# Reordering the start of a chunked linear recurrence in a fused attention and mixture-of-experts kernel

## The chip, the cores and the metric

The kernel runs on one core of a Trainium2 chip. The metric is the device time of one execution in microseconds (us). The engines are named as in the profile: PE is the matrix engine (PEld its weight loads), DVE the vector engine, ACT the scalar engine, POOL the GpSimd engine, SP the engine whose queue issues most DMAs. Each engine works through its own list of instructions strictly in order and waits on semaphores for the others.

## The reference, cut to what matters

Four batches with eight heads give 32 independent recurrences over 768 steps, with a 40x40 state each. The result, laid out as 3072 tokens of 320 features, goes through a top-1 mixture of eight experts.

```python
def _attn_ref(r, k, v, w, a, b):
    for t in range(768):
        y[:, :, t] = einsum('bhd,bhde->bhe', rt, state)
        Sa = einsum('bhde,bhe->bhd', state, at)
        state = state * wt[:, :, None, :] - einsum('bhd,bhe->bhde', Sa, bt)
        state = state + einsum('bhd,bhe->bhde', vt, kt)

def _moe_ref(x, w_gate, w_output_gate, w1, w2):
    e_idx = argmax(x @ w_gate); gate_w = softmax(x @ w_gate)[e_idx]
    eom = sigmoid(x @ w_output_gate)
    for e in range(8):
        out[mask_e] = gate_w * eom * (relu(x[mask_e] @ w1[e]) @ w2[e])
```

## The kernel before, in words

The 768 steps are cut into 12 chunks of 64 (C). Inside a chunk the recurrence is a triangular system, so each chunk needs a preparation that doesn't depend on the state, an inverse of its triangular matrices, and then a sequential part that takes the state in and hands it on. The 32 heads lie as two sides of 16 (NP).

`scan(c)` (L104) loads the decays w of chunk c by a DMA on SP (L110), squares them on ACT for a range check (L112), and runs two prefix products P and I on DVE (L116), a reciprocal (L118) and a scaling of I (L120). `prep(c)` (L128) loads a, k and b (D, L135), forms the decayed Av on DVE (L176, L177, and two columns on ACT, L178), sends strips of it into LA by DMA (L171), forms KBt on DVE (L183), and copies Wp on ACT (L187). Then, for each of the two sides, it makes three masked copies Am of Av (for chunk 0 all six on DVE, L198; for the others on ACT, L200), and for three groups of that side multiplies them by KBt on PE (L206) into a PSUM tile pl. From each pl, ACT copies the LA part (L210), POOL cuts it to a triangle (L212), and two copies fill the two halves of N (L218: for chunk 0 the first half on DVE, otherwise both on ACT). After that come Nm (L165) and transposes of KBt and Wp on PE with copies on ACT (L155, L157). The tile Am has one buffer, or for side 1 of chunk 0 one of KB's; LA and KB have four buffers, so preparation of chunk c+4 waits for chunk c's readers.

`tinv(cs)` (L226) inverts the triangular blocks: transposes of N on DVE (L241, or L246 for pairs of chunks), a chain of multiply and reduce pairs on DVE (L251, L253, L287, L292, L295) each of which needs the one before, a last transpose (L303, or L308), and for the first four chunks (FAST) two copies Tc on ACT (L305). Chunks 0 to 3 are inverted singly, the others in pairs.

`crit(c, q)` (L339) is the sequential part for half q of the heads: the products of LA with the state (L350), masked moves on ACT (L354), applications of Tc, Nm and N on PE (L363) with additions on DVE (L376), the copies into XU on ACT (L393, L394), and the new state (L401 to L410), which is scaled by Dt, a product of LA of this chunk and of the next on POOL (L380). `tail` (L413) forms the outputs, and `route` and `pick` (L604, L625) the choice of expert. After the last chunk the experts run (L827).

What sets the order: the program is traced once in Python, a planner gives each instruction a priority by its place in that trace, and lays out every engine's list with its own estimates of when each instruction becomes ready, picking the ready instruction of highest priority. The trace order comes from `run` (L469). Its generator `background` traces scan 0, then for each batch of chunks prep, the next chunk's scan, and tinv; `need(c)` advances it until chunk c's inverse is traced, and four steps of it (RATE) are traced per step of `crit`:

```python
s.warm(s.ident, 40)
s.scan(0)
for b in batches:
    yield from preps(b)      # prep(c), then scan(c + 1)
    if b == batches[0]:
        first()              # loads of the router weights
    yield from inv(b)        # tinv(b)
```

`need(min(c + 1, n - 1))` (L522) stands ahead of crit(c, 0), so preparation and inverse of chunk 1 and the scan of chunk 2 are traced ahead of the sequential part of chunk 0.

Of the kernel before, what the change touches and what calls it, by code (L numbers as in the profile page):

```python
# [20 lines left out]
C = 64  # L21
NP = 16
# [32 lines left out]
class Att:  # L55
    npool = 0

    def __init__(s, ctx, tc, ident, win, din, rl, vl, vt, nch=12):
        s.tc, s.nc, s.nch, s.ident = tc, tc.nc, nch, ident
        s.win, s.din, s.rl, s.vl, s.vt = win, din, rl, vl, vt  # L60
        nc = s.nc
        pool = lambda n, b, **k: ctx.enter_context(tc.tile_pool(name=n, bufs=b, **k))
        s.cp, s.p2, s.p5 = (pool(f"p{i}", i) for i in (1, 2, 5))
        s.ps = pool("ps", 1, space=PSUM)
        s.dr = pool("dr", 2, space=DRAM)
        s.pre = ExitStack()
        s.p1 = s.pre.enter_context(tc.tile_pool(name="p0", bufs=1))
        s.mM = s.cp.tile([128, C], F32, name="mM")
        nc.gpsimd.memset(s.mM, 1.0)
        for h in range(2):  # L70
            nc.gpsimd.affine_select(out=s.mM[64 * h:64 * h + 64], in_=s.mM[64 * h:64 * h + 64], pattern=[[1, C]],
                                    base=0, channel_multiplier=-1, compare_op=ALU.is_gt, fill=0.0)

        s.mj = s.cp.tile([120, 3], F32, name="mj")
        nc.gpsimd.memset(s.mj, -1.0)
        for j in range(3):
            m = s.mj[:, j:j + 1]
            nc.gpsimd.affine_select(out=m, in_=m, pattern=[[0, 1]], base=-40 * j, channel_multiplier=1,
                                    compare_op=ALU.is_ge, fill=0.0)
            nc.gpsimd.affine_select(out=m, in_=m, pattern=[[0, 1]], base=40 * j + 39, channel_multiplier=-1,  # L80
                                    compare_op=ALU.is_ge, fill=0.0)
        s.rst = s.p1.tile([120, 792], BF16, name="rst")
        nc.gpsimd.memset(s.rst, 0.0)
        nc.gpsimd.memset(s.rst[:, 0:792:33], 1.0)
        s.Tt = s.p1.tile([128, 1056], F32, name="Tt")
        nc.gpsimd.memset(s.Tt, 0.0)
        nc.gpsimd.memset(s.Tt[:, 0:1056:33], 1.0)


        s.hm = s.cp.tile([128, 2], F32, name="hm")  # L90
        nc.vector.tensor_reduce(out=s.hm, in_=s.ident.rearrange("p (x h s) -> p h x s", x=4, h=2), axis=AX.XY, op=ALU.add)
        s.hq = s.cp.tile([128, 2], F32, name="hq")
        nc.vector.tensor_reduce(out=s.hq, in_=s.ident.rearrange("p (x h s) -> p h x s", x=2, h=2), axis=AX.XY, op=ALU.add)
        s.wb = s.cp.tile([120, 1], F32, name="wb")
        nc.gpsimd.memset(s.wb, -0.9)
        s.wsq = s.cp.tile([120, nch], F32, name="wsq")
        s.rqm = s.cp.tile([120, nch], F32, name="rqm")
        s.zb = s.cp.tile([128, 32], F32, name="zb")
        nc.gpsimd.memset(s.zb, 0.0)
        s.buffers()  # L100
        s.st, s.ld, s.post, s.idle = {}, {}, [], False


    def scan(s, c):  # L104

        nc, V = s.nc, s.nc.vector
        n = 12 * 2 * 33
        w = s.p1.tile([120, n + 1], F32, name="w")
        V.memset(w[:, n:], 0.0)
        nc.sync.dma_start(out=w[:, 0:n], in_=s.win[c])  # L110
        sq = s.p1.tile([120, 24, 32], BF16, name="sq")
        nc.scalar.activation(out=sq, in_=pat(w, 1, [(33, 24), (1, 32)]), func=AF.Square, bias=s.wb, accum_out=s.wsq[:, c:c + 1])  # L112
        P, I = (s.p1.tile([120, 12, 2, 33], F32, name=x) for x in "PI")
        Pf, If = (x.rearrange("p r h t -> p (r h t)") for x in (P, I))
        for o, d in ((Pf, w[:, 0:n]), (If[:, ::-1], w[:, n:0:-1])):
            V.tensor_tensor_scan(out=o, data0=d, data1=s.rst, initial=0.0, op0=ALU.mult, op1=ALU.add)  # L116
        rq = s.p1.tile([120, 24], F32, name="rq", bufs=2)
        V.reciprocal(out=rq, in_=P[:, :, :, 32])  # L118
        I3 = I.rearrange("p r h t -> p (r h) t")
        V.tensor_tensor(out=I3, in0=I3, in1=rq.unsqueeze(2).broadcast_to([120, 24, 33]), op=ALU.mult)  # L120
        s.Q = P, I, rq
# [6 lines left out]
    def prep(s, c):  # L128
# [60 lines left out]
        for side in range(2):  # L189
# [4 lines left out]
            else:  # L194
                Am = s.p1.tile([120, 3, 6, C], F32, name="Am", tag="Am")
            for j in range(3):
                if c == 0:
                    V.tensor_scalar(out=Am[:, j], in0=As_[:, :, 0:64], scalar1=s.mj[:, j:j + 1], scalar2=None, op0=ALU.mult)  # L198
                else:
                    nc.scalar.activation(out=Am[:, j], in_=As_[:, :, 0:64], func=AF.Copy, scale=s.mj[:, j:j + 1])  # L200
            yield
            for g0 in range(0, 6, 2):
                pl = s.ps.tile([128, 2, 3, C], F32, name="pl", tag="pl" if c or g0 == 0 else "tl", bufs=2 if c or g0 == 0 else 3)
                nj = 3 if g0 < 4 else 2
                for i in range(2):
                    nc.tensor.matmul(pl[:, i, 0:nj], KBt[:, 6 * side + g0 + i].rearrange("p n t -> p (n t)"), Am[:, 0:nj, g0 + i],  # L206
                                     start=True, stop=True)
                pv = pl.rearrange("p g j t -> p j g t")
                la = pat(LA[64:128, side], 66 * g0, [(396, nj), (66, 2), (1, 64)])
                nc.scalar.copy(out=la, in_=pv[0:64, 0:nj])  # L210
                for i in range(2):
                    g.affine_select(out=la[:, :, i], in_=la[:, :, i], pattern=[[0, nj], [1, C]], base=0, channel_multiplier=-1,  # L212
                                    compare_op=ALU.is_gt, fill=0.0)
                for h in range(2):
                    r = slice(64 * side + 32 * h, 64 * side + 32 * h + 32)
                    n = C - 32 * h
                    nn = pat(N[r], C * g0, [(6 * C, nj), (C, 2), (1, n)])
                    (V.tensor_copy if c == 0 and not h else nc.scalar.copy)(out=nn, in_=pv[64 + 32 * h:96 + 32 * h, 0:nj, :, C - n:])  # L218
                yield
        split()  # L220
        for side in range(2):
# [4 lines left out]
    def tinv(s, cs):  # L226
# [73 lines left out]
            s.st[c]["Tc"] = s.Tp[:, c % 2]  # L300
        if fast:
            Th = tmp[:, 512:1024].rearrange("p (n x t) -> p n x t", x=2, t=16)
            V.transpose(out=pat(Th, 0, [(1, 16), (16, 2), (32, NP)]), in_=pat(Tt, 0, [(1, 16), (0, 2), (32, 16)]))  # L303
            for x in range(2):
                nc.scalar.activation(out=s.st[cs[0]]["Tc"][:, :, 16 * x:16 * x + 16], in_=Th[:, :, x], func=AF.Copy,  # L305
                                     scale=s.hm[:, x:x + 1])
# [162 lines left out]
    def run(s, sink, first, then=None):  # L469
# [17 lines left out]
        def background():  # L487
            s.warm(s.ident, 40)
            s.scan(0)
            for b in batches:  # L490
                yield from preps(b)
                if b == batches[0]:
                    first()
                yield from inv(b)
            s.pre.close()
            s.idle = True
            if then:
                yield from then()
# [551 lines left out]
```

## Time and profile before

| | us |
|---|---|
| median of 3 runs | 797.86 |
| lowest and highest | 795.27, 801.42 |
| profiled execution | 804.69 |
| its span, first to last instruction | 803.0 |

All instruction times are those of the profiled execution, counted from the start of its span; 1.69 us of its time lie outside the span. In the timeline view, a line is a start, a duration, the engine, the source line, the operation, what it writes and reads, how many instructions were merged, and in brackets the idle time of that engine just before and what ended it. A group of merged instructions lasts from the first start to the last end.

### The profile page before, as it was taken

What the parts mean: (1) busy time and instruction counts of PE and PEld (TensorE: products, weight loads), DVE (VectorE), ACT (ScalarE), POOL (GpSimd) and SP (SyncE); (2) the same over time, 40 slices, a digit from 0 to 9 for tenths busy, and PEclk for the clock granted to TensorE, in tenths of its full rate; (3) what the DMA queues carried; (4) which work ended last, traced back from release to release, by engine and by line L of the source; (5) the groups of instructions that cost most, each with busy time, mean ns of one, the idle gap of its engine ahead of it and who ended that gap; (6) DMA issues with size and microseconds to landing.
All of it is one profiled execution on the core that took longest, in us unless ns stands there. A gap on an engine that the chain in (4) does not pass through costs nothing. (4 is left out here: it accounts for less than half of the span.)

```text
span 803.0 us, 22193 instructions
## 1 busy us (share of the span) xinstructions
PE 687.7 (86%) x9378; PEld 616.9 (77%) x9378; DVE 472.2 (59%) x921; ACT 386.9 (48%) x871; POOL 231.2 (29%) x334
## 2 busy tenths in 40 slices
PE   5767987876898798889999968978999999999992
PEld 5656767765787687778888867767899998988992
DVE  7877766257952568946975954335467454455220
ACT  1576684665325783765387323424356253353210
POOL 9541223313112234452132320022534223311101
PEclk9555699999779988997999989898999999999997
DMA  7653334244222544364431554206557335332001
GB/s 173 149 119 81 95 89 105 72 99 108 69 56 57 116 105 106 93 130 96 100 83 46 112 123 126 62 13 171 173 169 215 120 106 184 108 93 67 16 9 28
DMA packets 61152, 81.13 MB, mean 101 GB/s; under 512 B 34226, under 2 KB 48373, under 8 KB 59606
## 3 DMA queue, kind: packets, MB, share of 16 engines
q1 hardware_dynamic: 57206, 70.74, 35.1%
q0 software_dynamic: 3840, 8.91, 3.8%
q8 instruction: 76, 1.25, 0.7%
q14 instruction: 30, 0.25, 0.1%
HBM read 67.59 MB, written 8.96 MB: 95 GB/s over the span
## 5 line engine op out<-in xcount | busy, mean ns | idle before, releaser
L212 POOL TENSOR_SCALAR_AFFINE_SELECT LA<-LA 64x192 f32<-64x192 f32 x144 | 69.7, 511 | 148.0 <-ACT LA L210 141.6
L206 PE MATMUL pl<-Am,KBt 120*128 120x192 f32 (+1 forms) x288 | 71.4, 396 | 24.6 <-ACT Am L200 16.4
L773 DVE SCALAR_TENSOR_TENSOR hl<-ph,hh 128x480 fp32r<-128x480 f32 (+1 forms) x76 | 41.7, 562 | 68.1 <-ACT hh L772 65.1
L768 PE MATMUL ph<-xh,w1h 128*128 128x480 f32 (+1 forms) x228 | 79.5, 353 | 2.3 <-DVE hl L773 1.3
L206 PEld LDWEIGHTS pl<-Am,KBt 120*128 120x128 f32 x288 | 56.8, 239 | 30.1 <-ACT Am L200 18.0
L781 PE MATMUL po<-w2h,hh 128*120 128x320 f32 x256 | 78.7, 312 | 1.1 <-ACT hh L772 1.1
L772 ACT ACTIVATE hh<-ph 128x480 fp32r<-128x480 f32 (+1 forms) x76 | 36.7, 498 | 88.6 <-PE ph L768 79.4
L768 PE MATMUL ph<-xl,w1h 128*128 128x480 f32 (+1 forms) x228 | 78.5, 347 | 0.0
L782 PE MATMUL po<-w2l,hh 128*120 128x320 f32 x256 | 77.6, 309 | 0.0
L783 PE MATMUL po<-w2h,hl 128*120 128x320 f32 x256 | 74.8, 310 | 0.0
L786 POOL DMA_INDIRECT out_dram<-y,ti x32 | 34.0, 1061 | 141.8 <-DVE y L785 75.8
L354 ACT ACTIVATE As<-pa,hq 128x320 f32<-128x320 f32 x88 | 46.3, 529 | 46.9 <-PE pa L363 33.8
L363 PE MATMUL pa<-As,Tc 64*32 64x40 f32 x2048 | 59.0, 212 | 9.5 <-ACT As L354 5.6
L363 PEld LDWEIGHTS pa<-As,Tc 64*32 64x32 f32 x2048 | 48.1, 118 | 20.6 <-ACT As L354 8.2
L452 PE MATMUL pY<-KB,M 128*64 128x40 f32 x768 | 57.3, 238 | 7.4 <-POOL M L443 4.3
L451 PE MATMUL pY<-Sd,R 128*64 128x40 f32 x704 | 57.1, 240 | 3.1 <-ACT LG L616 3.1
L435 PE MATMUL pM<-R,VU 128*128 128x128 f32 x384 | 57.3, 302 | 1.8 <-ACT VU L427 1.7
L452 PEld LDWEIGHTS pY<-KB,M 128*64 128x64 f32 x768 | 50.0, 147 | 9.7 <-POOL M L443 4.5
L218 ACT COPY N<-pl 32x192 f32<-32x192 f32 (+1 forms) x138 | 49.9, 362 | 10.1 <-PE pa L363 7.7
L687 POOL DMA_INDIRECT tab<-rec,si x24 | 25.5, 1063 | 99.0 <-DVE rec L684 49.9
L435 PEld LDWEIGHTS pM<-R,VU 128*128 128x128 f32 x384 | 51.2, 210 | 3.5 <-ACT VU L427 2.1
L451 PEld LDWEIGHTS pY<-Sd,R 128*64 128x64 f32 x704 | 48.3, 146 | 6.6 <-ACT LG L616 3.3
(192 smaller groups left out, 1645.2 us busy)
## 6 DMA issues: line engine op xcount, KB each, us to landing
D<-in_din_dram SPq DMA_DIRECT2D x12, 1080.0 KB
st<-in_w_dram SPq DMA_DIRECT2D x16, 512.0 KB
st<-in_w_dram SPq DMA_DIRECT2D x16, 480.0 KB
XS<-in_vt_dram SPq DMA_DIRECT2D x24, 256.0 KB
XU<-in_vt_dram SPq DMA_DIRECT2D x24, 256.0 KB
VU<-in_vl_dram SPq DMA_DIRECT2D x24, 208.0 KB
w<-in_win_dram SPq DMA_DIRECT2D x12, 371.2 KB
st<-in_w_dram SPq DMA_DIRECT2D x16, 256.0 KB
```

The costliest lines, as they stand in the source:

```text
L206: nc.tensor.matmul(pl[:, i, 0:nj], KBt[:, 6 * side + g0 + i].rearrange("p n t -> p (n t)"), Am[:, 0:nj, g0 + i], start=True, stop=True)
L212: g.affine_select(out=la[:, :, i], in_=la[:, :, i], pattern=[[0, nj], [1, C]], base=0, channel_multiplier=-1, compare_op=ALU.is_gt, fill=0.0)
L218: (V.tensor_copy if c == 0 and not h else nc.scalar.copy)(out=nn, in_=pv[64 + 32 * h:96 + 32 * h, 0:nj, :, C - n:])
L354: nc.scalar.activation(out=x, in_=pa, func=AF.Copy, scale=s.hq[:, h:h + 1])
L363: nc.tensor.matmul(pa[o + w:o + w + 32, i], m(p)[o:o + 64], x[o:o + 64, i, :], start=start, stop=True, tile_position=(o, o + w), skip_grou ...
L435: nc.tensor.matmul(pM[:, i], VU[:, h0 + i].rearrange("p n t -> p (n t)"), R[:, :, h0 + i], start=True, stop=True)
L451: nc.tensor.matmul(o, R[:, side, i, :], Sd[:, i, :], start=True, stop=False)
L452: nc.tensor.matmul(o, Ms[i // 4][:, i % 4, side, :], KB[:, side, p, :], start=not c, stop=True)
L768: nc.tensor.matmul(ph, l, r, start=(i == 0), stop=(i == 7))
L781: nc.tensor.matmul(po, hh[f][:, ts_], w2h[:, f], start=(f == 0), stop=False)
L782: nc.tensor.matmul(po, hh[f][:, ts_], w2l[:, f], start=False, stop=False)
L783: nc.tensor.matmul(po, hl[f][:, ts_], w2h[:, f], start=False, stop=(f == 7))
```

## The change

`issue_after(ins)` makes each instruction traced in its block that runs on the engine of `ins` stand behind `ins` in that engine's list; it adds no wait and binds no other engine. `high_priority()` lets what is traced in it go ahead of all else that is ready.

The change traces prep(0) and tinv(0) under high priority, and the scan of chunk 1 and the router's loads only after them. The three masks of side 1 of chunk 0 go from DVE to ACT. Each scan's DVE instructions get a place to stand behind: scan 1 stands behind the last DVE copy of chunk 0's N; scans 2 to 5 stand behind the last DVE transpose of the inverse of chunks 0 to 3. In every chunk and group N's two copies are traced ahead of the copy into LA.

```diff
@@ Att.__init__
-        s.st, s.ld, s.post, s.idle = {}, {}, [], False
+        s.st, s.ld, s.post, s.idle, s.mark = {}, {}, [], False, {}
     def scan(s, c):
+        with s.tc.issue_after(s.mark[c]) if c in s.mark else ExitStack():
+            s.scan_(c)
+    def scan_(s, c):
@@ prep
             for j in range(3):
-                if c == 0:
+                if c == 0 and not side:
                     V.tensor_scalar(out=Am[:, j], in0=As_[:, :, 0:64], scalar1=s.mj[:, j:j + 1], ...)
                 else:
                     nc.scalar.activation(out=Am[:, j], in_=As_[:, :, 0:64], func=AF.Copy, scale=s.mj[:, j:j + 1])
@@
+                for h in range(2):
+                    r = slice(64 * side + 32 * h, 64 * side + 32 * h + 32)
+                    n = C - 32 * h
+                    nn = pat(N[r], C * g0, [(6 * C, nj), (C, 2), (1, n)])
+                    pn = pv[64 + 32 * h:96 + 32 * h, 0:nj, :, C - n:]
+                    if c == 0 and not h:
+                        s.mark[1] = V.tensor_copy(out=nn, in_=pn).ins
+                    else:
+                        nc.scalar.copy(out=nn, in_=pn)
                 nc.scalar.copy(out=la, in_=pv[0:64, 0:nj])
                 for i in range(2):
                     g.affine_select(out=la[:, :, i], ...)
-                for h in range(2):
...
-                    (V.tensor_copy if c == 0 and not h else nc.scalar.copy)(out=nn, ...)
@@ tinv
-            V.transpose(out=pat(Th, ...), in_=pat(Tt, ...))
+            s.mark[cs[0] + 2] = V.transpose(out=pat(Th, ...), in_=pat(Tt, ...)).ins
@@ run, background
             s.scan(0)
-            for b in batches:
+            for g in (s.prep(0), s.tinv([0])):
+                while True:
+                    with s.tc.high_priority():
+                        if next(g, done) is done:
+                            break
+                    yield
+            ready[0] = True
+            s.scan(1)
+            first()
+            for b in batches[1:]:
                 yield from preps(b)
-                if b == batches[0]:
-                    first()
                 yield from inv(b)
```

## Rows read from the trace of the kernel before

**Rows 1.** The page's busy times of the engines over the whole span, and the granted clock of PE in 40 equal slices of 20 us (tenths of full speed).
```profile
PE 687.7 (86%) x9378; PEld 616.9 (77%) x9378; DVE 472.2 (59%) x921; ACT 386.9 (48%) x871; POOL 231.2 (29%) x334
...
PEclk9555699999779988997999989898999999999997
```

**Rows 2.** Busy time of each engine by stretch: stretch, its length, then for each engine the busy us and the count, the granted clock, the DMA share and GB/s. The stretches are from the first mask product to the end of chunk 0's Tc, from there to chunk 0's first XU copy, and from there to the last XU copy.
```profile
20.30:58.70 38.40, 26.66 (x136) 21.70 (x136) 28.78 (x51) 24.65 (x64) 18.91 (x30) 0.50 0.62 139
58.70:87.30 28.60, 20.68 (x273) 17.66 (x274) 20.67 (x50) 19.83 (x48) 4.93 (x12) 0.56 0.26 65
87.30:525.00 437.70, 378.08 (x7202) 333.31 (x7202) 282.06 (x580) 241.23 (x577) 111.34 (x170) 0.90 0.39 94
```

**Rows 3.** Timeline of DVE from 17 to 40 us: chunk 0's masks, scan 1, chunk 1's KBt, the first transpose of inverse 0.
```profile
17.25 7.36 DVE L198 TENSOR_SCALAR Am<-Av,mj 120x384 f32<-120x384 f32 x6
24.54 1.79 DVE L116 TENSOR_TENSOR_SCAN P<-w,rst 120x792 f32<-120x792 f32 x1
26.25 1.88 DVE L116 TENSOR_TENSOR_SCAN I<-w,rst 120x792 f32<-120x792 f32 x1
...
31.98 0.98 DVE L120 TENSOR_TENSOR I<-I,rq 120x792 f32<-120x792 f32 x1
...
38.25 0.95 DVE L183 TENSOR_TENSOR KBt<-D,I 120x768 f32<-120x768 f32 x1
39.12 1.09 DVE L241 STREAM_TRANSPOSE tmpf<-N 128x512 f32<-128x512 f32 x1
```

**Rows 4.** The view of line 198 alone: duration of one mask on DVE, least, median and greatest, in ns.
```profile
L198 DVE TENSOR_SCALAR Am<-Av,mj x6: 401/1390/2087, 17.2 to 24.2; 120x384 f32<-120x384 f32 x6
```

**Rows 5.** Timeline of POOL beside these masks: three clears of LA for later chunks.
```profile
18.08 5.99 POOL L139 MEMSET LA<- 32x2112 f32 x3
```

**Rows 6.** Timeline of ACT: the Square of scan 1, the LA copies behind it, the last copies of chunk 0's N and of chunk 1's N, the masks of chunk 2 and Tc of chunk 0.
```profile
23.81 0.94 ACT L112 ACTIVATE sq<-w,wb 120x768 bf16<-120x768 f32 x1 [7.38 <-DMA w<-in_win_dram]
...
24.86 0.85 ACT L210 COPY LA<-pl 64x384 f32<-64x384 f32 x2
...
37.24 0.47 ACT L218 COPY N<-pl 32x192 f32<-32x192 f32 x2
...
55.60 0.63 ACT L218 COPY N<-pl 32x256 f32<-32x256 f32 x2
56.26 1.62 ACT L200 ACTIVATE Am<-Av,mj 120x384 f32<-120x384 f32 x3
57.79 0.89 ACT L305 ACTIVATE Tc<-tmpf,hm 128x256 f32<-128x256 f32 x2
```

**Rows 7.** Timeline of PE: the 24 matmuls of chunk 0's pl (side 0 is the first row), and the first application of Tc.
```profile
20.33 3.78 PE L206 MATMUL pl<-Am,KBt 120*128 120x192 f32 x12 [4.22 <-DVE Am L198]
24.67 2.93 PE L206 MATMUL pl<-Am,KBt 120*128 120x192 f32 x8 [0.56 <-DVE Am L198]
...
33.01 1.22 PE L206 MATMUL pl<-Am,KBt 120*128 120x128 f32 x4
...
58.73 1.28 PE L363 MATMUL pa<-As,Tc 64*32 64x40 f32 x32 [1.92 <-ACT Tc L305]
```

**Rows 8.** Groups of instructions by line, costliest first: busy us, mean ns of one, idle time before. ACT's copies of LA and N, and its masks.
```profile
L218 ACT COPY N<-pl 32x192 f32<-32x192 f32 (+1 forms) x138 | 49.9, 362 | 10.1 <-PE pa L363 7.7
...
L200 ACT ACTIVATE Am<-Av,mj 120x384 f32<-120x384 f32 x66 | 35.9, 605 | 0.4
...
L210 ACT COPY LA<-pl 64x384 f32<-64x384 f32 (+1 forms) x72 | 31.2, 437 | 16.7 <-PE pl L206 15.3
```

**Rows 9.** Timeline of DVE in the inverses of chunks 0 and 1: the scans of chunks 2 and 3 inside them, Av of chunk 2, and each inverse's last transpose.
```profile
41.80 1.81 DVE L116 TENSOR_TENSOR_SCAN I<-w,rst 120x792 f32<-120x792 f32 x1 [0.30 <-ACT Wp L187]
...
43.58 1.80 DVE L116 TENSOR_TENSOR_SCAN P<-w,rst 120x792 f32<-120x792 f32 x1
...
49.09 0.57 DVE L176 TENSOR_TENSOR Av<-D,I 120x396 f32<-120x396 f32 x1 [0.24 <-ACT Am L200]
...
52.95 1.07 DVE L303 STREAM_TRANSPOSE tmpf<-Tt 128x512 f32<-128x512 f32 x1
...
58.71 1.08 DVE L241 STREAM_TRANSPOSE tmpf<-N 128x512 f32<-128x512 f32 x1 [4.69 <-ACT Tc L305]
...
65.43 1.80 DVE L116 TENSOR_TENSOR_SCAN I<-w,rst 120x792 f32<-120x792 f32 x1
...
67.32 1.80 DVE L116 TENSOR_TENSOR_SCAN P<-w,rst 120x792 f32<-120x792 f32 x1
...
73.64 1.07 DVE L303 STREAM_TRANSPOSE tmpf<-Tt 128x512 f32<-128x512 f32 x1
```

**Rows 10.** The view of line 393 alone: the first XU copies of the 24 half chunks (least, median and greatest duration in ns, first and last start).
```profile
L393 ACT COPY XU<-pa x24: 416/418/422, 87.3 to 524.9; 64x320 f32<-64x320 f32 x24
```

**Rows 11.** The view of line 308 alone, columns likewise: the last transposes of the four paired inverses.
```profile
L308 DVE STREAM_TRANSPOSE Tc<-Tt x4: 1942/1970/1990, 226.0 to 467.7; 128x1024 f32<-128x1024 f32 x4
```

**Rows 12.** Who waited for whom between 130 and 525 us, total, times and longest: POOL's clear of a later chunk's LA behind the products that read the buffer.
```profile
POOL LA L139 <- PE pa L350: 13.4, 5, 4.9
```

**Rows 13.** Timeline of PE late in chunk 0: an application of Tc, 32 matmuls like that of rows 7.
```profile
113.72 0.76 PE L363 MATMUL pa<-As,Tc 64*32 64x40 f32 x32
```

**Rows 14.** Busy time by stretch, columns as in rows 2: two stretches in which the granted clock changes.
```profile
80.00:85.00 5.00, 3.11 (x65) 2.59 (x59) 2.18 (x4) 4.57 (x12) 1.21 (x4) 0.84 0.14 47
...
100.00:120.00 20.00, 16.46 (x285) 13.91 (x279) 11.99 (x27) 16.76 (x40) 4.24 (x11) 0.91 0.33 89
```

More of the change, by code (lines that the diff above doesn't have):

```diff
@@ L213, in prep @@
                                     compare_op=ALU.is_gt, fill=0.0)
-                for h in range(2):
[L215 to L218, printed above, removed]
                 yield
@@ L302, in tinv @@
             Th = tmp[:, 512:1024].rearrange("p (n x t) -> p n x t", x=2, t=16)
-            V.transpose(out=pat(Th, 0, [(1, 16), (16, 2), (32, NP)]), in_=pat(Tt, 0, [(1, 16), (0, 2), (32, 16)]))
+            s.mark[cs[0] + 2] = V.transpose(out=pat(Th, 0, [(1, 16), (16, 2), (32, NP)]),
+                                            in_=pat(Tt, 0, [(1, 16), (0, 2), (32, 16)])).ins
             for x in range(2):
```

## The prediction, made before the changed kernel ran

> **What bounds the kernel now.** I read the page first: PE is busy 86% of the span, no other engine over 60%, and its granted clock is at half for slices 2 to 4, from 20 to 80 us [rows 1]. Busy time by stretch then parts the program in two. From 20.3 to 87.3 us PE is busy 47 of 67 us (71%), most of it at half clock, DVE 49 and ACT 44: no engine is full, so the order of the work and its waits bound it [rows 2]. From the first XU copy at 87.3 to the last at 525 PE is busy 378 of 438 us, 86% [rows 10, 2]. The change touches the first part, and the timelines of DVE, ACT, POOL and PE there say what stands in whose way.
>
> The chain to chunk 0's sequential part runs: masks, products pl on PE, copies into N, inverse, Tc, first application of Tc at 58.73 [rows 7]. Four things stretch it. (a) The six masks take 7.36 us on DVE although one takes 0.40 when undisturbed and 2.09 beside POOL's clears of LA, which last from 18.08 to 24.07 [rows 3 to 5]. (b) Scan 1 stands behind them on DVE, from 24.54 to 28.13, and its Square held ACT's list for 7.38 us until its load landed, so the first LA copy, ready when side 0's products were, starts at 24.86 [rows 3, 6]. (c) N is whole only at 37.71 (37.24 + 0.47), the last products having run at 33.01, and the inverse starts at 39.12, behind chunk 1's KBt [rows 6, 7, 3]. (d) Scan 2 and Av of chunk 2 sit inside inverse 0, and Tc waits on ACT behind the masks of chunk 2, to end at 58.68 [rows 9, 6].
>
> **The change part by part.** *Masks.* Side 0 keeps its three on DVE; PE started on it at 20.33 and I leave that [rows 7]. High priority may put chunk 0's clears ahead of others on POOL, and the clears of LA could move: 2 us either way at most, one clear's length (5.99/3) [rows 5]. Side 1's three cost 3 x 0.605 = 1.8 us on ACT [rows 8], idle until 23.81; they are done by 20 if the Square isn't ahead of them, and at 24.8 + 1.8 = 26.6 if it is [rows 6]. DVE gets 4.1 us back (two clears' worth), but nothing may use it: scan 1 is held behind N.
>
> *N ahead of LA, scan 1 behind N.* Side 0's products end at 24.11; side 1's last 2.93 + 1.22 = 4.15 and follow at once, to 28.3 [rows 7]. Per group ACT then owes 0.36 (half of N) before 0.44 (LA) [rows 8], less than PE's 1.3 per group, so N is whole at 29.0 instead of 37.71: 8.7 earlier. With the Square ahead of the masks side 1 runs from 26.6 and N is whole at 31.5; with everything as good as the masks on side 0 allow, 28.6. LA's triangle on POOL comes 0.4 later per group in every chunk; POOL is busy 29% [rows 1], so I cost it at nothing, and at 0.4 a chunk, 5 us in all, if POOL's triangle were what the sequential part waits for.
>
> *Inverse 0.* It ran from 39.12 to 54.02, 14.9 us. Inside are scan 2 (1.81 + 1.80, and 0.98 for the scaling as in scan 1), a pair of Av (2 x 0.57) and 0.54 of waiting: 6.2 [rows 9, 3]. Its own work is thus 8.7. After the change scan 2 can't enter, but scan 1 can: it is ready when N's last DVE copy is issued, and high priority only helps an instruction that is ready, while each step of the inverse waits for the one before. I let scan 1's 4.6 in and chunk 1's Av and KBt not: 29.0 + 8.7 + 4.6 = 42.3, Tc at 43.2 (0.89 on ACT [rows 6]). That is 15.5 earlier than 58.68. With nothing inside, 38.6 (20.1 earlier). With Av and KBt inside too (2 x 0.57 + 2 x 0.95 = 3.0) and Tc's ACT wait kept (57.79 - 54.02 = 3.8), 50.0 (8.7 earlier).
>
> *Chunk 1.* This pays. Its scan ran while DVE was otherwise waiting; now it starts at 29.0 and competes with inverse 0. Chunk 1's KBt ended at 39.20 [rows 3]. It would end at 29.0 + 4.6 + 3.0 = 36.6 ahead of the inverse, 45.3 wholly behind it. I take 41, nearer the middle since they interleave: 2 later. N of chunk 1 goes from 56.23 [rows 6] to 58.2. Inverse 1 before stood 2.5 us behind that (58.71), because Tc of chunk 0 was late on ACT; this goes. It lasted 16.0 us with scan 3 inside, which is now behind it: 11.4 [rows 9]. So it ends at 58.4 + 11.4 = 69.8 rather than 74.71: 5 earlier (bounds 9 earlier, 1 later).
>
> *Later scans.* Scans 4 and 5 leave inverses 2 and 3 in the same way: 4.6 each for the inverse, and as much against the next chunk's preparation. I count them as zero, bounds plus or minus 4.6.
>
> *What reaches the end.* Chunk 0's sequential part is 15.5 earlier at its start, chunk 1's inverse 5. The first XU copy (87.3) lies between, since its steps share every list with chunk 1 and 2's preparation: I take 10, the middle. It is carried on: LA has four buffers and POOL's clear for a later chunk waits for the products that read the buffer [rows 12], and the last paired inverse ends at 469.7, 55 us before the last XU copy [rows 11, 10], so preparation and sequential part pull each other along. Sum on the profiled execution: 804.7 - 10 = 794.7. The three timed runs have their median 6.8 lower, at 797.9; the same 10 off that gives **788**, its own range 783 to 793.
>
> *The clock.* PE is granted 0.50 from 20 to 80 us [rows 1], with holes of up to 4.2 us ahead of its products [rows 7], then 0.84 in 80 to 85, and 0.91 over 100 to 120 with 82% busy [rows 14]: 1.2 GHz first, 2.4 GHz later. I leave the same stretch of the list at the same level. The Trainium skill (TensorE: Matmul & The Clock Gate, section What's actually happening) has the slow level as the default that activity releases; by that rule a start with fewer holes would get 2.4 GHz earlier, and the first rival below follows; the trace agrees in that the level rises where the holes close.
>
> **The rivals.** *The full clock comes with chunk 0.* 32 applications take 1.28 us at half clock and 0.76 later [rows 7, 13]. A half chunk of chunk 0 applies Tc four times, Nm twice, N once: 7 x 0.52 = 3.6 off its way. For it: the holes go. Against: 20 us of PE's 67 from 20.3 to 87.3 are idle [rows 2], more than chunk 0's own holes, and chunk 1's remain. Time 784.
>
> *Given back in the long stretch.* From 87 to 525 PE is busy 86% [rows 2]; if it is PE's list that sets that pace, an earlier chunk 0 only idles for PE until the rest is prepared, and what is won is the one hole that chunk 0's N made, 33.01 - 27.60 less what other work filled, about 3 [rows 7]. For it: the busy share. Against: 60 us of idle in that stretch, and buffers that tie preparation to the sequential part. Time 795.
>
> *Chunk 1 starves: slower.* If the planner lets inverse 0 run whole ahead of scan 1, chunk 1's KBt ends 6.1 late (45.3). Inverse 1 then runs from 62.7 to 74.1, and scan 3, now behind it, ends at 78.7 where it ended at about 70.4 (67.32 + 1.80 + 1.3 [rows 9]): 8.3 late. Scan 5 behind inverse 3 adds the same increase again, 2.2: 10.5 later in all, if preparation paces the sequential part. It decides from about 5 us of lateness in chunk 1's KBt, where inverse 1's gain is gone. For it: DVE is idle but for three copies from 20.3 to 28.3 in the new order, which the old one filled. Against: preparation had its own slack, Tc of chunk 0 being last. Time 808.
>
> *The change doesn't do what it says.* The new edges bind DVE alone. Square and load of scan 1 stay free, and priority ranks only what is ready by the planner's own estimates; lists may come out much as they were, with only the two clears' worth of masks gone, 4.1. Time 794.
>
> **How the numbers follow.** Forecast 0.46, of which 0.34 over 1% faster (1% is 8 us, about what a measurement of this kernel can tell from no change) and 0.12 within; full clock 0.10, faster; given back 0.20, of which 0.04 over 1% slower; chunk 1 starves 0.16, of which 0.13 slower; no more than the masks 0.08, 0.02 faster, 0.05 within, 0.01 slower. That makes 0.46 faster, 0.36 within 1%, 0.18 slower. The range reaches from all bounds good together with the clock (Tc 20.1 earlier, carried whole, with 3.6: 774) to just under the starved case (806).
>
> **What would show it.** Right: products pl of side 1 straight behind side 0's, N whole by 29 to 32, Tc of chunk 0 by 39 to 50, no scan inside inverses 0 to 3 but scan 1, first XU copy by 73 to 82, and the last XU copy earlier by about as much. Wrong: N of chunk 1 after 62; a first XU copy earlier by ten and a last one that isn't; a Square that still holds ACT's list ahead of side 1's masks.

## The result, and the profile after

The changed kernel took 807.8 us (median, 804.3 to 811.5) beside 798.5 for the kernel before (795.3 to 801.4): a ratio of 1.0133, 95% interval 1.0089 to 1.0177. It is slower, by some 10 us; the forecast was 788. The profiled executions took 811.5 and 804.7, above the medians of their kernels by different amounts, so a difference of 2 us between the two profiles is not read. Ratios here and below are those on record, which leave out runs well above the fastest of their kernel (five of m2's ten), so a ratio need not be that of the two medians.

The page of the changed kernel, in the form of [rows 1]: PE's share fell by a point, and the clock's half level, at 20 to 80 us before, now comes back in slice 6, from 100 to 120 us.

```profile
PE 684.6 (85%) x9378; PEld 616.9 (76%) x9378; DVE 469.9 (58%) x918; ACT 384.3 (47%) x874; POOL 227.1 (28%) x334
...
PEclk9656957979889988999999969998899999999997
```

Busy time by stretch, columns as in [rows 2]: from the first mask product to the end of chunk 0's Tc, to the first XU copy, to the last one. The first two are together 13.1 us shorter (53.9 for 67.0), the third is 15.1 longer (452.8 for 437.7) for nearly the same busy time of PE (381.4 for 378.1). What was won at the start was lost behind it.

```profile
23.74:51.10 27.36, 18.70 (x120) 15.79 (x121) 21.37 (x44) 19.75 (x50) 10.86 (x16) 0.62 0.68 149
51.10:77.60 26.50, 19.53 (x269) 16.78 (x269) 20.92 (x44) 19.71 (x51) 10.86 (x18) 0.63 0.35 89
77.60:530.40 452.80, 381.44 (x7221) 337.24 (x7220) 285.47 (x591) 243.76 (x591) 105.95 (x176) 0.89 0.38 91
```

ACT at the start, beside [rows 6]: side 1's masks now stand behind the Square of chunk 1, which waits 8.64 us for its load; N is whole at 34.02 (37.71 before); Tc stands behind three masks of chunk 1 and ends at 51.07 (58.68).

```profile
26.67 0.94 ACT L117 ACTIVATE sq<-w,wb 120x768 bf16<-120x768 f32 x1 [8.64 <-DMA w<-in_win_dram]
...
27.61 1.61 ACT L205 ACTIVATE Am<-Av,mj 120x384 f32<-120x384 f32 x3
...
33.76 0.26 ACT L223 COPY N<-pl 32x128 f32<-32x128 f32 x1
...
48.65 1.62 ACT L205 ACTIVATE Am<-Av,mj 120x384 f32<-120x384 f32 x3
50.18 0.89 ACT L315 ACTIVATE Tc<-tmpf,hm 128x256 f32<-128x256 f32 x2
```

DVE, beside [rows 3, 9]: scan 1 lies between N and the inverse (36.10), KBt of chunk 1 inside it, scan 2 behind its last transpose.

```profile
31.95 1.83 DVE L121 TENSOR_TENSOR_SCAN P<-w,rst 120x792 f32<-120x792 f32 x1
...
36.10 1.07 DVE L250 STREAM_TRANSPOSE tmpf<-N 128x512 f32<-128x512 f32 x1
...
39.57 0.94 DVE L188 TENSOR_TENSOR KBt<-D,I 120x768 f32<-120x768 f32 x1
47.00 1.07 DVE L312 STREAM_TRANSPOSE tmpf<-Tt 128x512 f32<-128x512 f32 x1
47.98 1.80 DVE L121 TENSOR_TENSOR_SCAN P<-w,rst 120x792 f32<-120x792 f32 x1
```

PE, beside [rows 7]: side 1's products follow side 0's only after a wait for ACT's masks.

```profile
23.74 3.78 PE L211 MATMUL pl<-Am,KBt 120*128 120x192 f32 x12 [6.37 <-DVE Am L203]
29.27 2.01 PE L211 MATMUL pl<-Am,KBt 120*128 120x192 f32 x12 [1.74 <-ACT Am L205]
...
53.18 1.14 PE L373 MATMUL pa<-As,Tc 64*32 64x40 f32 x26
```

The XU copies and the paired inverses' last transposes, as in [rows 10, 11]. The first XU copy is 9.7 earlier, the last 5.5 later; the last transpose of the first paired inverse starts 5.3 later.

```profile
L403 ACT COPY XU<-pa x24: 417/417/421, 77.6 to 530.4; 64x320 f32<-64x320 f32 x24
```
```profile
L318 DVE STREAM_TRANSPOSE Tc<-Tt x4: 1918/1970/2002, 231.3 to 465.2; 128x1024 f32<-128x1024 f32 x4
```

Where the lead goes is seen half chunk by half chunk. Read from ACT's timeline and DVE's, start times in us (an inverse by the start of its last transpose):

```
                    XU 1   XU 2   XU 3   XU 7   XU 24 | scan 5  scan 6  inverse 0, 1, 2, 3
before              87.3  120.9  138.4  242.5  524.9 | 118.7   166.4   53.0  73.6  99.8 130.8
changed             77.6  109.0  139.1  244.1  530.4 | 118.2   169.7   47.0  68.2  95.7 117.3
late scans alone    74.7  111.2  137.9  241.7  519.1 | 122.7   167.8   47.4  68.5  99.2 121.7
```

All of the lead of 10 to 12 us is gone at the third copy. PE's timeline suggests why: ahead of the first half chunk's products pS stand 124 matmuls of the preparation (72 pl, 52 transposes) before and 104 (68 and 36) in the changed kernel; ahead of the third stand 176 (104 and 72) in both. So the first XU copy came earlier with chunk 0's Tc (7.6 earlier) and with 20 preparation matmuls that only went behind it. The preparation itself is hardly earlier: scan 5 starts at 118 in both, because it now waits for the inverse that it used to sit in.

The loss shows much later. The same copies towards the end, with five runs that are explained below:

```
                 XU 13   XU 19   XU 20   XU 21   XU 24
before           360.6   451.8   462.8   482.6   524.9
changed          361.1   450.8   467.4   496.2   530.4
e1               367.0   458.4   475.3   501.6   531.8
h1               352.9   442.2   452.6   481.8   509.5
h2               362.0   448.7   465.9   489.0   525.6
z1               340.9   428.6   439.7   457.0   491.9
z2               332.8   420.8   438.2   466.5   498.8
```

At the 19th copy the changed kernel is 1.0 ahead, at the 21st 13.7 behind, and it keeps 5.5 of that to the last.

### The profile page after: what moved, and what is told of

It is laid out like the page before. It is cut to its first block, busy times and chain, and to the rows that moved or that the text cites. A ratio compares the mean times of both kernels' runs of the same rounds, so it can differ in the third digit from the quotient of the medians.

```text
span 809.6 us, 22196 instructions
## 1 busy us (share of the span) xinstructions
PE 684.6 (85%) x9378; PEld 616.9 (76%) x9378; DVE 469.9 (58%) x918; ACT 384.3 (47%) x874; POOL 227.1 (28%) x334
## 5 line engine op out<-in xcount | busy, mean ns | idle before, releaser
L211 PE MATMUL pl<-Am,KBt 120*128 120x192 f32 (+1 forms) x288 | 71.0, 396 | 23.8 <-ACT Am L205 14.1
L226 POOL TENSOR_SCALAR_AFFINE_SELECT LA<-LA 64x192 f32<-64x192 f32 x144 | 59.6, 444 | 101.7 <-ACT LA L224 89.0
L211 PEld LDWEIGHTS pl<-Am,KBt 120*128 120x128 f32 x288 | 57.3, 240 | 28.6 <-ACT Am L205 15.9
L373 PE MATMUL pa<-As,Tc 64*32 64x40 f32 x2048 | 56.6, 209 | 14.2 <-ACT As L364 8.1
L462 PE MATMUL pY<-KB,M 128*64 128x40 f32 x768 | 57.3, 239 | 12.2 <-POOL M L453 8.2
L373 PEld LDWEIGHTS pa<-As,Tc 64*32 64x32 f32 x2048 | 46.2, 116 | 24.2 <-ACT As L364 9.8
L704 POOL DMA_INDIRECT tab<-rec,si x24 | 31.8, 1324 | 102.6 <-DVE rec L701 59.4
L785 PE MATMUL ph<-xh,w1l 128*128 128x480 f32 (+1 forms) x152 | 53.6, 353 | 0.0
```

The costliest lines, as they stand in the source:

```text
L373: nc.tensor.matmul(pa[o + w:o + w + 32, i], m(p)[o:o + 64], x[o:o + 64, i, :], start=start, stop=True, tile_position=(o, o + w), skip_grou ...
L462: nc.tensor.matmul(o, Ms[i // 4][:, i % 4, side, :], KB[:, side, p, :], start=not c, stop=True)
L785: nc.tensor.matmul(ph, l, r, start=(i == 0), stop=(i == 7))
```

## The experiments

Each ratio is to the kernel before, run on the same chip in between. The letters in the expectations: A, the lists that come with chunk 0 first, in which ACT's casts of the first expert's weights stand ahead of half chunk 21's moves and wait for their loads; B, the late scans starve the preparation; C, N ahead of LA delays LA; D, the Squares, which wait for w at the head of ACT's list; E and F are told where they come.

**Which part loses?** Each part of the change alone on the kernel before, then combinations.

e1, chunk 0 first with side 1's masks on ACT:

```diff
-            for b in batches:
+            for g in (s.prep(0), s.tinv([0])):   # each step under high_priority()
...
-                if c == 0:
+                if c == 0 and not side:
```

> Kernel before with chunk 0's preparation and inverse traced first under high priority and side 1's masks on ACT; scans free, LA copied ahead of N. Theory A (the end is set late: in ACT's list of the changed kernel all three casts of expert 0's first weights stand ahead of half chunk 21's XU copy, one of them ahead of its first move, and each waits for its load): this kernel has the same order there, so the first XU copy comes 5 to 12 us earlier than before, half chunk 21's XU copy 8 to 15 us later, and the time is 803 to 812. Rival B (scans held behind inverses and N starve chunk 1 and the later chunks): this kernel has none of that, so it is no slower than before, 788 to 799. Rival C (N ahead of LA in every chunk delays LA): also 788 to 799.

e2, scans 2 to 5 behind the inverses (`s.mark[cs[0] + 2] = V.transpose(...)`), nothing else:

> Kernel before with scans 2 to 5 alone queued behind the inverses of chunks 0 to 3. Theory A: the casts stand in ACT's list nearly as in the kernel before (one ahead of half chunk 21's XU copy), so the time is that of before, 792 to 803, whatever the start gains or loses. Rival B: slower, 803 to 812. Rival C: 792 to 803.

e3, N's two copies ahead of LA's, nothing else:

> Kernel before with N's copies ahead of LA's copy in every chunk and nothing else. Theory A: one cast ahead of half chunk 21's XU copy as in the kernel before, time 792 to 803. Rival B: 792 to 803. Rival C: slower, 803 to 812, with more waiting for LA in the chunks after the first.

e4, the changed kernel with LA ahead of N again:

> Changed kernel with LA's copy ahead of N's again, all else kept. Theory A: the casts stand as in the changed kernel, time 803 to 812. Rival B: 803 to 812. Rival C: back to that of before or faster, 788 to 799.

f1, e2 and e3 together, that is the change without chunk 0 first, its masks and scan 1's place:

> The kernel before with N ahead of LA and scans 2 to 5 behind the inverses, the Squares left where they are. If the two parts add: 790 to 796. If chunk 0 first was needed for the half clock at 107 to 137 us: granted clock 1.00 over 105 to 140; if late scans alone bring it on, as they did by themselves: under 0.85 there. If the waits for w set the time: their sum 28 to 31 us and a time of 790 to 794.

```
e1  811.9 us  1.0171 [1.0086, 1.0256]        e4  806.8 us  1.0060 [1.0014, 1.0107]
e2  797.6 us  1.0006 [0.9964, 1.0048]        f1  792.1 us  0.9951 [0.9907, 0.9995]
e3  794.6 us  0.9956 [0.9916, 0.9996]
```

All kernels with chunk 0 first and its masks are slower, and A's times fit all four of e1 to e4. B falls: late scans alone cost nothing. C falls as the cause: N first alone gains a little, and e4, without it, is still slower. Beside the changed kernel (1.0133) e4 is if anything the faster, with intervals that overlap, so N first is not shown to gain there. f1 lies 1.8 points of the ratio below the changed kernel. Late scans also tell what an early first XU copy is worth: e2 and f1 have theirs at 74.7 and 76.1, earlier than the changed kernel, and their third at 137.9 and 138.7.

Then e1's two halves (for these two, and k1b, the cause was still open):

> The kernel before with chunk 0's preparation and inverse first, and nothing else: all six masks stay on VectorE, scans and copies as before. Together with the masks on ScalarE it took 811.9. If the order alone brings the loss: 805 to 815, w's first load late again (scan 0 at 11 to 12 us where it was 10.0), first XU copy 77 to 86. If the masks on ScalarE are needed for it (the Square that waits ahead of them): 794 to 801.

> The kernel before with side 1's three masks of chunk 0 on ScalarE, and nothing else; here they stand ahead of Square 1 in ScalarE's list. If the masks on ScalarE bring the loss: 803 to 812. If the loss needs chunk 0 first (masks behind the Square that waits for w): 790 to 799, side 1's masks done by 20 us, N of chunk 0 whole 2 to 4 us earlier than before's 37.7.

m1, the masks alone: 800.4, 0.9995 [0.9954, 1.0037]. m2, chunk 0 first alone: 804.2, 1.0004 [0.9944, 1.0065], but its ten runs spread from 791.8 to 812.7, and their median is 0.7% above the other's. Both medians lie between the two ranges put down for them. So the masks alone cost nothing that shows, the order alone is undecided, and the two together cost 1.7%. ACT's timeline shows a difference between m1 and e1. In m1 the masks stand ahead of the Square:

```profile
16.57 1.63 ACT L200 ACTIVATE Am<-Av,mj 120x384 f32<-120x384 f32 x3
...
23.48 0.94 ACT L112 ACTIVATE sq<-w,wb 120x768 bf16<-120x768 f32 x1 [5.29 <-DMA w<-in_win_dram]
```

In e1 behind it:

```profile
27.47 0.94 ACT L112 ACTIVATE sq<-w,wb 120x768 bf16<-120x768 f32 x1 [8.86 <-DMA w<-in_win_dram]
...
28.41 1.61 ACT L200 ACTIVATE Am<-Av,mj 120x384 f32<-120x384 f32 x3
```

Whether this one stall makes the two together dear was not tried by itself.

**The order of the casts (A).** h1 gives the kernel before the changed kernel's late order of the casts at half chunk 21, h2 takes it from the changed one:

```diff
+            with s.tc.issue_after(s.casts[k]) if (c, q) == (10, 0) and k < 3 else ExitStack():   # h1
...
+                s.tc.add_manual_dep(s.casts[(0, 0, 1, 2)[k]], ins.name, ...)                     # h2
```

> Kernel before, with only this: in ACT's list the first three moves of half chunk 21 stand behind the three casts of expert 0's first weights, the order that the changed kernel has there. Theory A (that order, in which ACT's sequential moves wait for weight loads, costs the changed kernel its lateness after 450 us): half chunk 21's XU copy comes 4 to 12 us later than in the kernel before, nothing earlier moves, time 802 to 808. Rival B (the lateness comes from the start, by chunk 1's or the scans' preparation): no change, 795 to 802.

> Changed kernel, with only this: the three casts stand behind the first move, the third move and the XU copy of half chunk 21, the order of the kernel before. Theory A: half chunk 21's XU copy comes 4 to 12 us earlier than in the changed kernel, time 797 to 803, that of before within 0.5%. Rival B: no change against the changed kernel, 804 to 811.

h1 took 792.3 (0.9952 [0.9905, 0.9998]), h2 810.6 (1.0233 [1.0161, 1.0305]). The step between copies 20 and 21 moved as wanted (29.2 us in h1, 23.1 in h2), the time did not follow. For the kernel before A falls: h1 has the late order and is not slower. h2 is no such test. Its copies 19 and 21 are still 40.3 us apart (45.4 in the changed kernel, 30.7 before), for in PE's list too work of the experts has come forward: their first transposes of gathered tokens (px) wait for the gather ahead of half chunk 21's applications, in h2 for 5.47 us. In the changed kernel they stand between its first applications of Tc:

```profile
478.56 0.74 PE L373 MATMUL pa<-As,Tc 64*32 64x40 f32 x14
484.04 0.66 PE L762 MATMUL px<-ident,xg 120*128 120x120 f32 x2 [4.74 <-DMA xg<-xd,ti]
484.63 0.47 PE L373 MATMUL pa<-As,Tc 64*32 64x40 f32 x6
```

Before, they come behind its last ones:

```profile
480.46 1.28 PE L363 MATMUL pa<-As,Tc 64*32 64x40 f32 x32
...
484.27 0.42 PE L745 MATMUL px<-ident,xg 120*128 120x120 f32 x2
```

Of the traces of these 20 kernels, ten have px ahead of copy 21, and copies 19 and 21 lie 39.6 to 45.8 us apart in them; the other ten have 25.0 to 31.2. Every kernel whose interval lies above the kernel before (the changed one, e1, e4, g1, h2) is among the first ten. So are h1, m1, m2, k3 and z2, which are not shown to be slower than the kernel before: the late lists go with the loss and, by h1 and m1 above all, do not make it by themselves. A run that moves px alone was not made.

**The Squares (D).** z1 and z2 leave out the Square of each scan and its sums (the check of w's range) from the changed kernel and from the one before:

```diff
-        nc.scalar.activation(out=sq, in_=pat(w, 1, [(33, 24), (1, 32)]), func=AF.Square, bias=s.wb, accum_out=...)
```

> Changed kernel without the Squares of the decays (they feed only a range check), so that no ACT instruction waits for a load of w. Its list of ACT has one cast ahead of half chunk 21's second move, as in the kernel before. Theory A: no late loss; and if the Square that waits for its load at 126 us is what paces half chunk 3 (theory D: it holds ACT's list ahead of a tail's copy, on which PE's list waits), the start's 8 to 12 us are kept at half chunk 3's XU copy (130 us or less) and the time is 785 to 795. Rival to D (preparation paces it by DVE and PE, not by this wait): half chunk 3's XU copy stays at 136 to 141. Rival B: 803 to 811.

> Kernel before without the Squares. Its list of ACT has all three casts ahead of half chunk 21's XU copy, one ahead of its first move, as in the changed kernel. Theory A: the step from half chunk 20 to 21 is 25 us or more (19.7 in the kernel before), time 799 to 810 unless the missing waits give it back. Rival B: 788 to 799, no longer than before, and no longer a step there.

z1 took 772.2 (0.9735 [0.9665, 0.9805]), z2 778.0 (0.9789 [0.9735, 0.9844]), both less than any range put down for them. Without the Squares the changed order takes 4.0 points of the ratio less (some 32 us), the old one 2.1 (some 17), and the changed one is then not the slower. But z1 is without the late px and z2 has it: z1 is 7.8 behind z2 at copy 19 and 6.9 ahead at the last, so this pair does not set the Squares apart from the late lists. One point of D missed: z1's lead at the first XU copy (74.4 for 80.8) was gone at the third all the same (133.8 for 132.9).

g1 to g3 keep the Squares and were to move them behind their scans:

```diff
+        rec = V.reciprocal(out=rq, in_=P[:, :, :, 32])
+        with s.tc.issue_after(rec.ins):
+            nc.scalar.activation(out=sq, ...)
```

> The changed kernel with each Square bound behind its own scan's reciprocal, so that it stands in ScalarE's list where its load of w has long landed; all work is kept. Theory D (the Squares that wait for w at the head of ScalarE's list carry the loss; with the Squares left out the changed kernel took 772.2): 773 to 784, ScalarE's wait for w under 8 us where it was 40, and no longer behind the old order with the same move. Rival E (it is the Square's busy time, 12 x 1.12 = 13.4 us on ScalarE, that costs, and not the wait): over 790. Rival F (the new order itself starves the preparation): 9 us or more above the old order with the same move, wherever both lie. First XU copy 74 to 78 in any case.

> The kernel before with the Squares bound behind their scans in the same way. Theory D: 778 to 788 (778.0 without the Squares, and their busy time off the path), ScalarE's wait for w under 8 us where it was 36. Rival E: 790 or more. The step between this and the changed kernel with late Squares: within 6 us either way by theory D, over 9 by rival F.

> The kernel before with N copied ahead of LA, scans 2 to 5 behind the inverses (0.9 and 3.9 us on their own), and the Squares late, without chunk 0 first. Theory D with parts that add: 773 to 782, the fastest of these four, below the kernel before by 2 to 3%. If N first and the late scans only helped because they shortened the Squares' waits (33.5 and 29.7 where the kernel before has 36.2), it is no faster than the kernel before with late Squares alone, 778 to 788.

g1 809.7 (1.0113 [1.0031, 1.0194]), g2 796.9 (0.9981 [0.9948, 1.0014]), g3 792.5 (0.9967 [0.9920, 1.0015]): nothing moved. The edit was a miss, not the theory: the mark is a VectorE instruction and binds VectorE's list alone, so the Squares on ScalarE stayed and waited as long as ever (31.4 us in g1). k1 to k3 mark ScalarE's own copy out of the scan:

```diff
+        av = nc.scalar.copy(out=Av[:, :, 64:66], in_=P[:, :, :, 32])
+        with s.tc.issue_after(av.ins):
+            nc.scalar.activation(out=sq, ...)
```

> The changed kernel with each Square issued behind ScalarE's copy of P into Av of the same chunk, so that w has landed when it heads the list; all work is kept. Theory D (the waits carry the loss): 774 to 788, no wait of a Square for w, and not slower than the kernel before by more than 0.5%. Rival E (the Squares' work costs, 1.12 us each ahead of N's copies on ScalarE, or the wait only moves to the copy into Av): 797 to 812, with ScalarE's idle time ahead of that copy up by 15 us or more. First XU copy 72 to 77 in either case.

> The changed kernel with each Square behind the copy into Av, once more. If the changed order costs nothing of its own once the Squares don't wait: 779 to 787, a ratio to the kernel before of 0.978 to 0.986, its interval over that of the order before with the same move (0.975 to 0.988). If it keeps a cost of its own: 788 to 795.

> The kernel before with the Squares moved in the same way. Theory D: 778 to 789. Rival E: 793 to 802. By theory D the step from this to the changed kernel with the same move lies within 6 us either way; if the changed order costs something of its own beside the Squares, it is 8 or more.

> The kernel before with N copied ahead of LA, scans 2 to 5 behind the inverses, and the Squares moved behind the copy into Av. Theory D: 772 to 784, the fastest of these. Rival E: 788 to 796, as without the move of the Squares (792.1).

```
k1   785.6 us  0.9866 [0.9787, 0.9944]       k2  784.6 us  0.9817 [0.9751, 0.9883]
k1b  787.1 us  0.9887 [0.9849, 0.9924]       k3  785.1 us  0.9844 [0.9781, 0.9907]
```

With all work kept, the move takes 2.5 to 2.7 points off the changed kernel's ratio (some 20 us), 1.8 off the one before (some 14) and 1.1 off f1 (some 8). So the Squares that wait are dear in every order, and rival E, that it is their work, falls. That they carry the changed kernel's loss is not shown: 1.3 points lay between the two orders, 0.5 to 0.7 are left with the move, and by the intervals it can be none or all of the 1.3. k1b missed its range (a ratio of 0.978 to 0.986) by a little, k3 was not the fastest. And the changed kernel has the late px, k1 hasn't. These are the fastest versions of the study with all work kept, 1.1 to 1.8% below the kernel before; which of them is best is open.

ACT's groups by line show the waits go (busy us and mean ns, then idle time ahead of the group and what ended it; the expectations count the first load's start too, hence 36 and 40). The Squares, the copies into Av and rs read what the scans and w deliver. Before, their waits are 31.4 + 9.3 + 14.1 = 54.8 us:

```profile
L112 ACT ACTIVATE sq<-w,wb 120x768 bf16<-120x768 f32 x12 | 11.2, 936 | 31.4 <-DMA w<-in_win_dram 31.4
...
L178 ACT COPY Av<-P 120x24 f32<-120x24 f32 x12 | 2.8, 233 | 9.3 <-DVE P L116 4.7 <-DMA LA<-Av 4.6
L174 ACT ACTIVATE rs<-rq 120x24 f32<-120x24 f32 x12 | 2.7, 223 | 14.1 <-DVE w L109 12.2 <-DVE rq L118 1.8
```

The changed kernel, 49.3:

```profile
L117 ACT ACTIVATE sq<-w,wb 120x768 bf16<-120x768 f32 x12 | 11.2, 935 | 28.8 <-DMA w<-in_win_dram 28.8
...
L183 ACT COPY Av<-P 120x24 f32<-120x24 f32 x12 | 2.7, 227 | 0.1
L179 ACT ACTIVATE rs<-rq 120x24 f32<-120x24 f32 x12 | 2.7, 222 | 20.4 <-DVE rq L123 11.9 <-DVE w L114 8.3
```

k1, 10.7; in k2 they are 30.8:

```profile
L184 ACT ACTIVATE sq<-w,wb 120x768 bf16<-120x768 f32 x12 | 11.2, 934 | 0.0
...
L181 ACT COPY Av<-P 120x24 f32<-120x24 f32 x12 | 2.8, 231 | 1.0 <-ACT Tc L316 0.9
L177 ACT ACTIVATE rs<-rq 120x24 f32<-120x24 f32 x12 | 2.6, 221 | 9.7 <-DVE rq L121 9.7
```

The copies into Wp read the scans too, and in k1 one of their groups waits where in the changed kernel it has 0.0 (the other has 0.7 in both):

```profile
L193 ACT COPY Wp<-P 120x372 f32<-120x372 f32 x12 | 6.1, 510 | 10.6 <-DVE P L119 10.6
```

So 28.0 us of waits taken away gave some 20, and 24.0 gave some 14 (in k2 the waits at Wp stay at 1.9). From f1 to k3 20.8 went (54.4 to 33.6) and gave some 8: there is no fixed share. And the changed kernel waits no longer in sum than the one before, so the sum is not its loss; that it put work that others need behind the waits is one reading, and a single place shows what that looks like. In the changed kernel's timeline of all engines at 126 us, the Square waits 3.30, behind it stands a copy of M, POOL waits for that and PE for POOL.

```profile
125.97 0.94 ACT L117 ACTIVATE sq<-w,wb 120x768 bf16<-120x768 f32 x1 [3.30 <-DMA w<-in_win_dram]
...
126.91 0.56 ACT L452 COPY M<-pM 128x512 f32<-128x512 f32 x1
127.61 1.26 POOL L453 TENSOR_TENSOR M<-M,mM 128x512 f32<-128x512 f32 x1 [5.39 <-ACT M L452]
...
128.93 1.08 PE L462 MATMUL pY<-KB,M 128*64 128x40 f32 x16 [2.63 <-POOL M L453]
```

Which of the nine Squares behind the 28.8 us carries how much is not settled. The Trainium skill (Perfetto Trace Analysis, section Tensor Engine Instruction (MATMUL, LD_WEIGHTS)) has ScalarE as a strict first-in, first-out queue; these rows agree, in that ACT's masks of chunk 0, whose input was there from 19 us (VectorE read it then), start only at 27.61, behind the Square.

k1 also shows what the start was to be: with no Square ahead, ACT's masks run at 18.44, all 24 products in one go, and the first XU copy is at 71.7. There the lead is partly kept: third copy 130.8, for 132.8 in k2 and 138.4 before.

```profile
18.44 1.63 ACT L206 ACTIVATE Am<-Av,mj 120x384 f32<-120x384 f32 x3 [1.00 <-DVE Av L179]
```
```profile
23.16 5.21 PE L212 MATMUL pl<-Am,KBt 120*128 120x192 f32 x24 [6.64 <-DVE Am L204]
```

## Why the prediction was wrong

**Masks and N.** Named as a bound, "the Square could sit ahead" was the case: N whole at 34.0, not 29.0 and past the bound of 31.5, since PE got side 0's masks 3.4 us later too (23.74 for 20.33).

**Inverse 0.** The work inside it was right: 36.10 to 48.07 is 12.0 us, against 8.7 of its own and 3.0 of Av and KBt. Scan 1 stood ahead of it and, but for its scaling (0.98), not inside. Tc's wait on ACT (2.1) was kept. Tc ends at 51.1, 7.6 earlier than before, just outside the bounds (38.6 to 50.0), which did not add the late Square to the worst of the rest.

**Chunk 1.** Right to a us or two: KBt at 40.5 (41 put), N of chunk 1 whole at 57.3 (58.2), the inverse from 57.4 (58.4).

**What reaches the end: the step that failed.** The first XU copy came 9.7 earlier, as put (10), but by luck: 10 was the middle between 15.5 for Tc and 5 for inverse 1, which came 7.6 and 5.4 earlier. "It is carried on" is wrong: the lead was gone at the third copy (139.1 for 138.4), and the last came 5.5 late. The prediction saw the tie between preparation and sequential part and let the sequential part lead. The rows point to the preparation: scan 5 did not move, the first paired inverse came 5.3 later, and 20 of PE's preparation matmuls had only gone behind the first copy. e2 and f1 lost the same lead at the same place. That is the rival *given back*, but PE's stretch is no fuller than before (381 of 453 us). No run moves the preparation alone, so that it sets the pace is a reading of these rows.

**What no step had.** On top of a gain of nothing came a loss of some 10, and its cause stays open. In the profiled pair it arises between copies 19 and 21, long behind the changed kernel's last Square (357 us), where its lists have the experts' first work ahead of half chunk 21; but h1 has such lists and is not slower, and e1 is 6.4 late by copy 13. The Squares' waits, of which the prediction priced one, for chunk 0's masks, are there in either order: moving the Squares gains some 20 us in the changed and some 14 in the old, and whether that difference is the loss is not shown. Rival *starves* named the measured time (808) by luck: KBt of chunk 1 was never at the 45.3 that it needs, and late scans alone cost nothing.

**The clock.** "The same level" held at the start, with a little more than before (0.62 and 0.63 for 0.50 and 0.56, [rows 2]), so the rival *full clock* fell. By the rule of the Trainium skill cited in the prediction (TensorE: Matmul & The Clock Gate, section What's actually happening) fewer holes should raise it; these rows don't test that, since PE is busy 68 and 74% in them, and was 69 and 72% before. Nor did the trace before agree as plainly as the prediction had it: 80 to 85 us is granted 0.84 with PE busy 62% [rows 14], and a stretch without a hole stays at half:

```profile
32.00:44.00 12.00, 12.00 (x93) 10.04 (x92) 9.33 (x15) 9.14 (x26) 4.46 (x8) 0.50 0.50 127
```

What was not foreseen is how much half level there is from 107 to 137 us (a granted 0.61, for 0.97 before). Before, two of four stretches, and the changed kernel's four:

```profile
110.00:120.00 10.00, 8.03 (x158) 6.59 (x157) 8.46 (x20) 8.41 (x21) 1.15 (x4) 1.00 0.36 88
...
130.00:140.00 10.00, 8.52 (x246) 7.55 (x246) 3.61 (x8) 4.94 (x11) 1.89 (x2) 1.00 0.30 67
```
```profile
100.00:110.00 10.00, 6.70 (x117) 5.28 (x112) 6.15 (x16) 9.31 (x25) 2.23 (x7) 0.65 0.26 76
110.00:120.00 10.00, 10.00 (x88) 8.19 (x83) 9.51 (x24) 4.29 (x10) 0.00 (x0) 0.50 0.51 112
120.00:130.00 10.00, 6.87 (x147) 6.09 (x148) 4.88 (x10) 2.24 (x6) 4.05 (x3) 0.84 0.46 130
130.00:140.00 10.00, 8.79 (x191) 7.66 (x190) 1.47 (x3) 3.56 (x9) 0.79 (x1) 0.64 0.05 18
```

PE has holes at 100 to 110 (6.70 busy of 10) and runs the next 10 us full, but at half clock. e2 and f1 have a granted 0.70 and 0.69 from 107 to 137 and are not slower in the end, so it can account for lead lost by the third copy, not for the 10 us of loss by itself. Over a whole execution the clock goes with the time: 793.6 us at a mean granted clock of 0.915 and 803.5 at 0.890 are the same kernel before, and the changed kernel's four runs have 0.892 to 0.894. The two profiled executions have the same (0.892 and 0.893) and lie 6.8 us apart, so the clock is not the whole loss; its share was not measured.

## What to carry to other kernels

An earlier first result is worth something only if the work that paces the rest is earlier too: count, in the busiest engine's list, what stands ahead of the first, third and tenth milestone, before counting the lead as won. In a strict list, look for each instruction that waits for a load and ask what stands right behind it; a side calculation that nobody waits for belongs behind an instruction of its own engine that needs the same load anyway (here 1.8% from moving one instruction). A change of the start can turn the planner's lists at the other end: compare both ends, and when a run is to take an order away, check in its trace that every engine's list has lost it. An edge that orders instructions binds only the engine on which its mark runs.

## What the runs showed of the hardware

A stretch of PE that is full by the busy share can still be the slow one: 88 matmuls took the 10 us from 110 to 120 at a granted 0.50, where before 158 went through in 8.0 us at 1.00; what ran in it differed too. And the masks kept their uneven price on VectorE beside POOL's clears (median 2.09 us, the shortest 0.63), with half of them gone.
